# A list scheduler with new costs: a port lock, a delay between dependent operations, and query high parts on ScalarE

## The chip, the cores and the metric

The kernel runs on one core of one Trainium2 chip. The time is device microseconds of one execution. Five engines work beside each other, each through its own instructions in a fixed order: TensorE (PE, with its weight loads as PEld), VectorE (DVE), ScalarE (ACT), GpSimd (POOL) and SyncE (SP), which here mostly issues DMAs. An instruction whose operand is not ready holds up everything behind it on its engine. So the order that is written into the program decides who waits for whom.

## The reference, cut to what matters

```
scores = q @ k.T / 8 + bias            # 2 batches x 8 heads, 768 positions, head size 64
keep   = (key < n_global) or (0 <= query - key < n_local)
a      = exp(scores - max) / (sum + 1e-9)
x      = a @ v                          # 1536 tokens x 512
h      = relu(x @ w_in); x = (h * h) @ w_out           # 512 -> 2048 -> 512
xn     = x / sqrt(mean(x*x) + 1e-6) * rms_g
out    = (silu(xn @ w_gate) * (xn @ w_val)) @ w_out2   # 512 -> 1536 -> 512
```

## The kernel before, in words

Attention is cut into 16 slices: 4 chunks of 384 tokens times 4 pairs of heads. A slice has three tiles of 128 queries, 48 tiles in all. A tile runs through this chain: scores on PE (L931 in fp32 for the first eight slices, L939 from high and low parts for the last eight), bias and row minimum on DVE from PSUM (L949, with an accumulator read), exp with row sum on ACT (L953), sum plus 1e-9 on POOL (L957), reciprocal on DVE (L960), the scaling of one head on DVE and of the other on POOL (both L963), transposes on PE (L970), a copy to SBUF on ACT (L972), and the product with v on PE (L980). The result is split into a high part (ACT, L368) and a low part (DVE, L369).

For the last eight slices queries and keys, too, are split into high and low parts: `hi` writes high parts (L900, on the engine that QHI and KHI name), then DVE writes the low parts of the query (L888) and of the key (L891). Eight splits have two heads each, so there are 16 query high parts `qs` and 16 key high parts `kh`.

The weights are 68 blocks of 512 KB. Each comes by a DMA into `wraw`, and `expand` turns it into fp32 in `wbits`: one ACT instruction (L410) and four on DVE (L411, L413, L415, L418), each of which reads what the one before wrote. Then ACT writes the high part `M` (L368) and POOL or DVE the low part (L369). A matrix product is three PE instructions (L378 to L380: high by high, high by low, low by high). The first MLP follows each finished chunk (`first`: products, relu and square on ACT at L479 to L481, low part on DVE at L482), then the norm, then the gated MLP in Strassen-like products. Where PE would idle early on, short matmuls of ones fill the time (L1266).

The order is set by a planner, the class `Plan`. Every operation is recorded with its engine, a duration, the latency until another engine can use its result (`lat`), and what it reads and writes. `forward` is a list scheduler: it takes the ready operation with the earliest due time on the engine that is free first, and gives each a start. `solve` runs forward and backward several times and keeps the plan that ends first; `emit` then writes the instructions sorted by those starts. The durations are formulas (DVE, FAST, ACT, POOL1, POOL2). An operation with `port` set is one that uses the SBUF access shared by VectorE and GpSimd, and such operations were planned one after the other. POOL operations of the attention had `port=False`: the planner thought them free of it.

Of the kernel before, what the change touches and what calls it, by code (L numbers as in the profile page):

```python
# [16 lines left out]
ALU = mybir.AluOpType  # L17
# [35 lines left out]
AHEAD = (0, 0, 0, 3, 1, 1, 3, 3) + 8 * (1,)  # L53
QHI, KHI = "POOL", "POOL"
NSLACK = 0.5
# [18 lines left out]
class Plan:  # L74
# [33 lines left out]
    def solve(self):  # L108
        for o in reversed(self.ops):
            for q in o.succ:  # L110
                o.due = min(o.due, q.due - o.dur - (o.lat if q.eng != o.eng else 0.0))
        best = None
# [14 lines left out]
    def backward(self):  # L127
# [3 lines left out]
        for o in sorted(self.ops, key=lambda o: (-o.end, -o.n)):  # L131
            last = end
            for q in o.succ:
                last = min(last, q.late - (o.lat if q.eng != o.eng else 0.0))
            taken = busy.setdefault(o.eng, [])
            dur = o.end - o.start
            at = len(taken)
            for i, (a, b) in enumerate(taken):
                if b <= last - dur + 1.0e-9:
                    at = i  # L140
                    break
                last = min(last, a)
            taken.insert(at, (last - dur, last))
            o.late = last - dur
# [3 lines left out]
    def forward(self):  # L148
# [9 lines left out]
        while done < len(self.ops):  # L158
# [18 lines left out]
            else:  # L177
                o = heappop(ready[e])[2]
            if o.port:
                t = max(t, held)  # L180
# [19 lines left out]
            o.start = t  # L200
            o.end = t + o.dur + extra
            free[e] = o.end
            if o.port:
                held = o.end
            done += 1
            for q in o.succ:
                q.ready = max(q.ready, o.end + (o.lat if q.eng != e else 0.0))
                q.left -= 1
# [11 lines left out]

LAT = {"PE": 0.35, "DVE": 0.28, "ACT": 0.33, "POOL": 0.4, "SP": 2.6, "END": 0.0}
DVE = lambda n: 0.07 + n / 960
FAST = lambda n: 0.13 + n / 1920
ACT = lambda n: 0.07 + n / 1200
POOL1 = lambda n: 0.08 + n / 960
POOL2 = lambda n: 0.18 + n / 457
DMA = lambda kb: max(0.45, kb / 265.0)
# [34 lines left out]
class Mlp:  # L262
# [132 lines left out]
    def expand(self):  # L395
# [13 lines left out]
        bi = lambda: tl(bits).bitcast(I32)  # L409
        self.plan.add("ACT", ACT(512), lambda: nc.scalar.activation(tl(bits), f32(tl(raw)[:, :, 1]), AF.Abs), rr, rb)  # L410
        self.plan.add("DVE", FAST(512), lambda: v.tensor_scalar(  # L411
            out=tl(bits), in0=tl(bits), scalar1=LEAST, scalar2=MOST, op0=ALU.max, op1=ALU.min), rb, rb, port=True)
        self.plan.add("DVE", FAST(512), lambda: v.tensor_scalar(  # L413
            out=bi(), in0=bi(), scalar1=3, scalar2=0x3FFFFFF8, op0=ALU.logical_shift_left, op1=ALU.bitwise_and), rb, rb, port=True)
        self.plan.add("DVE", DVE(512) + 0.09, lambda: v.scalar_tensor_tensor(  # L415
            out=bi(), in0=tl(raw)[:, :, 0], scalar=29, in1=bi(), op0=ALU.logical_shift_right, op1=ALU.bitwise_or),
            rr + rb, rb, port=True)
        self.plan.add("DVE", DVE(512) + 0.09, lambda: v.scalar_tensor_tensor(  # L418
            out=bi(), in0=tl(raw)[:, :, 1], scalar=-(1 << 30), in1=bi(), op0=ALU.bitwise_and, op1=ALU.bitwise_or),
# [368 lines left out]
class Attention:  # L788
# [55 lines left out]
    def load(self, s):  # L844
# [18 lines left out]
        for j in range(2):  # L863
# [4 lines left out]
            if hp:  # L868
                self.op("POOL", 0.18 + CH / 985, lambda j=j, head=head: nc.gpsimd.tensor_scalar(
                    out=self.whole(s)[1][head, j], in0=self.whole(s)[1][head, j], scalar1=2.0 ** (2 * hp + j), scalar2=1.0,  # L870
                    op0=ALU.mult, op1=ALU.mult), [("qz", SLOTS[s])] + rq[j], rq[j], port=False)

    def split(self, s, kw):
# [9 lines left out]
        for j in range(2):  # L883
# [3 lines left out]
            self.hi(KHI, kw, lambda j=j: kh()[:, j, keys], lambda j=j: raw()[:, j, keys], 1.0, mine, [h] + whole)  # L887
            self.op("DVE", DVE(CH) + 0.09, lambda j=j, scale=scale: nc.vector.scalar_tensor_tensor(  # L888
                out=qs()[low, j], in0=raw()[low, j, KW:], scalar=scale, in1=f32(qs())[low, j],
# [5 lines left out]
    def hi(self, eng, n, out, src, scale, r, w):  # L895
# [3 lines left out]
        else:  # L899
            self.op(eng, 0.36 + n / 1830 if eng == "POOL" else FAST(n), lambda: self.mlp.eng(eng).tensor_scalar(  # L900
                out=out(), in0=src(), scalar1=scale, scalar2=1.0, op0=ALU.mult, op1=ALU.mult), r, w, port=eng == "DVE")

# [17 lines left out]
    def tile(self, n, due):  # L920
# [23 lines left out]
        for j in range(2):  # L944
# [398 lines left out]
```

## Time and profile before

| | us |
|---|---|
| median of 3 runs | 652.68 (652.17 to 653.1) |
| the profiled execution | 652.1 |
| its span, from the first instruction to the last | 650.2 |
| PE busy | 637.1 (98%) |
| DVE busy | 492.1 (76%) |
| ACT busy | 370.8 (57%) |
| POOL busy | 219.1 (34%) |

The 1.9 us between the span and the execution's time lie outside the program's instructions. The busy shares are averages over stages with different limits. A PE that is busy is not a PE at its peak, since the records of pipelined matmuls overlap. The rows that were read stage by stage stand further down.

### The profile page before, as it was taken

Reading aid. Unit: us, or ns where it says so; the run is one execution under the profiler, and the core shown is the slowest. Engines: PE = TensorE matmul, PEld = TensorE weight load, DVE = VectorE, ACT = ScalarE, POOL = GpSimd, SP = SyncE. Lnnn points to the kernel's source line nnn. Section 1 sums busy time; section 2 is a strip of 40 time slices with the busy share of each in tenths; the row PEclk is TensorE's granted clock in tenths of the full one; section 3 lists DMA queues with packets and bytes.
Section 4 is the critical chain, followed back from the end, with each engine's and each line's share of the span. In section 5 each row is a group of like instructions: output and inputs, shape, how many; then the busy total and the mean of one; then the engine's idle time right before and its main releaser. Section 6 shows DMA issues by size and latency. Waiting matters only on the chain.

```text
span 650.2 us, 10647 instructions
## 1 busy us (share of the span) xinstructions
PE 637.1 (98%) x3794; PEld 600.5 (92%) x3794; DVE 492.1 (76%) x1055; ACT 370.8 (57%) x834; POOL 219.1 (34%) x275
## 2 busy tenths in 40 slices
PE   8999999999999999999999999999999999999996
PEld 8788889899999999999999999999899999998995
DVE  6999998933888885237679998698878888887444
ACT  4779687766756564356656776654453443443310
POOL 5644666522332230024300212434454335351000
PEclk9999999999999999999999999999999999999998
DMA  8875676100333333002210110232121202310023
GB/s 228 234 234 152 195 180 168 49 25 7 125 123 104 99 118 109 0 1 76 87 34 1 33 33 1 66 105 89 38 94 66 98 32 77 119 65 1 2 85 115
DMA packets 20848, 56.38 MB, mean 87 GB/s; under 512 B 3248, under 2 KB 6064, under 8 KB 20784
## 3 DMA queue, kind: packets, MB, share of 16 engines
q1 hardware_dynamic: 19472, 53.82, 26.9%
q10 hardware_dynamic: 1312, 1.77, 0.8%
q8 instruction: 32, 0.52, 0.3%
q14 instruction: 32, 0.26, 0.1%
HBM read 52.43 MB, written 3.15 MB: 85 GB/s over the span
## 4 chain that ended last, share of the span: by engine, by line
PE 81%; DVE 12%; ACT 3%; DMA 2%; issue 1%; POOL 0%; SPq 0%; ACTq 0%; DVEq 0%; POOLq 0%
PE b L378 26%; PE b L379 26%; PE b L380 26%; DVE p L949 2%; DVE p L963 1%; PE tb L970 1%; PE av L980 1%; PE ps L939 1%; DVE kl L891 1%; DVE wbits L415 1%; DMA q<-in_kq_dram 1%; DVE wbits L418 1%; ACT p L953 1%; DVE wbits L413 1%; DMA k<-in_kq_dram 1%
## 5 line engine op out<-in xcount | busy, mean ns | idle before, releaser
L369 POOL TENSOR_TENSOR M<-wbits,M 128x512 fp32r<-128x512 f32 x60 | 82.0, 1372 | 226.5 <-ACT M L368 139.6
L378 PE MATMUL b<-xh,M 128*128 128x384 f32 x336 | 115.7, 344 | 0.5 <-DVE xl L369 0.5
L379 PE MATMUL b<-xl,M 128*128 128x384 f32 x336 | 112.8, 336 | 0.0
L380 PE MATMUL b<-xh,M 128*128 128x384 f32 x336 | 112.7, 335 | 0.0
L482 DVE TENSOR_TENSOR h<-ra,h 128x384 fp32r<-128x384 f32 x64 | 38.4, 604 | 44.7 <-ACT ra L481 44.5
L368 ACT CAST M<-wbits 128x512 fp32r<-128x512 f32 x68 | 41.8, 617 | 43.2 <-DVE wbits L418 29.9
L378 PEld LDWEIGHTS b<-xh,M 128*128 128x128 f32 x336 | 63.2, 188 | 2.7 <-DVE xl L369 0.8
L379 PEld LDWEIGHTS b<-xl,M 128*128 128x128 f32 x336 | 63.2, 188 | 1.9 <-DVE xl L369 0.3
L380 PEld LDWEIGHTS b<-xh,M 128*128 128x128 f32 x336 | 63.1, 188 | 0.2 <-DVE M L369 0.2
L378 PE MATMUL b<-h,M 128*128 128x384 f32 x176 | 61.0, 346 | 0.0
L665 DVE TENSOR_TENSOR y<-b,y 128x512 f32<-128x512 f32 (+1 forms) x61 | 41.2, 679 | 24.1 <-PE b L380 23.7
L379 PE MATMUL b<-h,M 128*128 128x384 f32 x176 | 59.1, 336 | 0.0
L380 PE MATMUL b<-h,M 128*128 128x384 f32 x176 | 59.0, 335 | 0.0
L380 PE MATMUL b<-M,h 128*128 128x512 f32 (+1 forms) x146 | 57.2, 392 | 0.0
L415 DVE SCALAR_TENSOR_TENSOR wbits<-wraw,wbits 128x512 int32<-128x512 int32 x68 | 56.1, 827 | 1.3
L379 PE MATMUL b<-M,h 128*128 128x512 f32 (+1 forms) x146 | 56.9, 390 | 0.0
L378 PE MATMUL b<-M,h 128*128 128x512 f32 (+1 forms) x146 | 56.8, 389 | 0.1
L953 ACT ACTIVATE p<-p,few 128x256 f32<-128x256 f32 (+1 forms) x96 | 46.4, 485 | 17.1 <-DVE few L949 13.9
L410 ACT ACTIVATE wbits<-wraw 128x512 f32<-128x512 f32 x68 | 45.1, 668 | 16.5 <-DMA wraw<-in_w_out_dram 8.5
L479 ACT ACTIVATE ra<-b 128x384 f32<-128x384 f32 x64 | 31.0, 486 | 39.6 <-PE b L380 39.4
L418 DVE SCALAR_TENSOR_TENSOR wbits<-wraw,wbits 128x512 int32<-128x512 int32 x68 | 50.3, 742 | 0.9
L411 DVE TENSOR_SCALAR wbits<-wbits 128x512 f32<-128x512 f32 x68 | 36.8, 541 | 9.7 <-ACT wbits L410 9.6
(137 smaller groups left out, 1616.5 us busy)
## 6 DMA issues: line engine op xcount, KB each, us to landing
wraw<-in_w_out_dram SPq DMA_DIRECT2D x28, 512.0 KB, 3.4
wraw<-in_w_in_dram SPq DMA_DIRECT2D x16, 512.0 KB, 3.5
wraw<-in_w_gate_dram SPq DMA_DIRECT2D x12, 512.0 KB, 3.3
wraw<-in_w_val_dram SPq DMA_DIRECT2D x12, 512.0 KB, 3.5
raw<-in_kq_dram SPq DMA_DIRECT2D x16, 240.0 KB, 4.8
raw<-in_kq_dram SPq DMA_DIRECT2D x16, 208.0 KB, 4.9
v<-in_vab_dram SPq DMA_DIRECT2D x8, 384.0 KB, 3.7
v<-in_vab_dram SPq DMA_DIRECT2D x8, 256.0 KB, 4.4
```

Of the source, the lines that this page charges most:

```text
L368: self.op("ACT", ACT(n), lambda: nc.scalar.copy(dst()[0], src()), rs, [(x, "hi") for x in ws])
L369: self.op(eng, t(n), lambda: e.tensor_tensor(out=dst()[1], in0=src(), in1=f32(dst()[0]), op=ALU.subtract), rs + [(x, "hi") for x in ws], [ ...
L378: nc.tensor.matmul(ps, lhsT=wh, rhs=ah, start=first, stop=False, skip_group_check=True)
L379: nc.tensor.matmul(ps, lhsT=wh, rhs=al, start=False, stop=False, skip_group_check=True)
L380: nc.tensor.matmul(ps, lhsT=wl, rhs=ah, start=False, stop=last, skip_group_check=True)
L410: self.plan.add("ACT", ACT(512), lambda: nc.scalar.activation(tl(bits), f32(tl(raw)[:, :, 1]), AF.Abs), rr, rb)
L411: self.plan.add("DVE", FAST(512), lambda: v.tensor_scalar(out=tl(bits), in0=tl(bits), scalar1=LEAST, scalar2=MOST, op0=ALU.max, op1=ALU.mi ...
L415: self.plan.add("DVE", DVE(512) + 0.09, lambda: v.scalar_tensor_tensor(out=bi(), in0=tl(raw)[:, :, 0], scalar=29, in1=bi(), op0=ALU.logica ...
L418: self.plan.add("DVE", DVE(512) + 0.09, lambda: v.scalar_tensor_tensor(out=bi(), in0=tl(raw)[:, :, 1], scalar=-(1 << 30), in1=bi(), op0=AL ...
L482: self.op("DVE", DVE(CH), lambda: nc.vector.tensor_tensor(out=get()[1], in0=t(), in1=f32(get()[0]), op=ALU.subtract), rt + hi, lo, port=True)
L665: self.op("DVE", DVE(a1 - a0), lambda o=o, ps=ps: nc.vector.tensor_tensor(out=o(), in0=ps(), in1=o(), op=ALU.add), [("b", bank)] + ro, ro)
L953: self.op("ACT", 0.29 + w / 1200, lambda j=j: nc.scalar.activation(tl(f"p{m}")[:, j, :w], tl(f"p{m}")[:, j, :w], AF.Exp, bias=tl("few")[:, ...
```

## The change

It has three parts. First, the planner's rules: a POOL operation with `port` now holds back or is held back through a lock that lies inside its own duration (it needs the lock `PRE` after its start and gives it back `POST` before its end), a dependent operation on the same engine is ready only `SAME` after the end of the one it reads (0.11 us on DVE, 0.12 on ACT, 0.08 on POOL, nothing on PE), and the POOL operations of the attention now have `port` set, all but L957. Second, new durations. Third, QHI names ACT: the 16 query high parts are written by an ACT instruction in place of a POOL one. What is computed stays the same. All lines from L226 on stand four lines lower in the changed kernel, so L963 is L967 there.

```
-QHI, KHI = "POOL", "POOL"
+QHI, KHI = "ACT", "POOL"
@@ solve, and backward in the same way
-                o.due = min(o.due, q.due - o.dur - (o.lat if q.eng != o.eng else 0.0))
+                o.due = min(o.due, q.due - o.dur - (o.lat if q.eng != o.eng else SAME[o.eng]))
@@ forward
-            if o.port:
+            lock = max(t + PRE, held) - t - PRE if o.port and e == "POOL" else 0.0
+            if o.port and e != "POOL":
                 t = max(t, held)
...
-            o.end = t + o.dur + extra
+            o.end = t + o.dur + extra + lock
             free[e] = o.end
             if o.port:
-                held = o.end
+                held = max(held, o.end - (POST if e == "POOL" else 0.0))
...
-                q.ready = max(q.ready, o.end + (o.lat if q.eng != e else 0.0))
+                q.ready = max(q.ready, o.end + (o.lat if q.eng != e else SAME[e]))
@@ durations
+SAME = {"PE": 0.0, "DVE": 0.11, "ACT": 0.12, "POOL": 0.08, "SP": 0.0, "END": 0.0}
+PRE, POST = 0.13, 0.12
-FAST = lambda n: 0.13 + n / 1920
+FAST = lambda n: 0.19 + n / 3600
-POOL2 = lambda n: 0.18 + n / 457
+POOL2 = lambda n: 0.14 + n / 461
+POOLS = lambda n: 0.25 + n / 1500
@@ hi (L900)
-            self.op(eng, 0.36 + n / 1830 if eng == "POOL" else FAST(n), lambda: self.mlp.eng(eng).tensor_scalar(
-                out=out(), in0=src(), scalar1=scale, scalar2=1.0, op0=ALU.mult, op1=ALU.mult), r, w, port=eng == "DVE")
+            self.op(eng, POOLS(n) if eng == "POOL" else FAST(n), lambda: self.mlp.eng(eng).tensor_scalar(
+                out=out(), in0=src(), scalar1=scale, scalar2=1.0, op0=ALU.mult, op1=ALU.mult), r, w, port=eng != "ACT")
@@ tile (L957, L960, L963)
-        self.op(EPS, 0.26, lambda: self.mlp.eng(EPS).tensor_scalar(
+        self.op(EPS, 0.19, lambda: self.mlp.eng(EPS).tensor_scalar(
...
-        self.op("DVE", 0.15, lambda: nc.vector.reciprocal(rs(), rs()), [("rs", m)], [("rs", m)])
+        self.op("DVE", 0.08, lambda: nc.vector.reciprocal(rs(), rs()), [("rs", m)], [("rs", m)])
...
-            self.op(e, 0.34 + w / 776 if e == "POOL" else FAST(w), lambda j=j, e=e: self.mlp.eng(e).tensor_scalar(
+            self.op(e, POOLS(w) if e == "POOL" else FAST(w), lambda j=j, e=e: self.mlp.eng(e).tensor_scalar(
...
-                op0=ALU.mult, op1=ALU.mult), [("rs", m), ("p", m, j)], [("p", m, j)], port=e != "POOL")
+                op0=ALU.mult, op1=ALU.mult), [("rs", m), ("p", m, j)], [("p", m, j)], port=True)
```

The new plan puts nearly everything in another order. Three places show how.

On VectorE, at the second weight block that is expanded, the kernel before has these rows. `p` are score tiles (a number for each of four buffers), `few` holds the row statistics, `wbits` and `wraw` the weight block, `M` its split form, and L949 with 128x1 is the accumulator read.

```order
L413 TENSOR_SCALAR wbits1_217<-wbits1_217 128x512
L960 RECIPROCAL few_157<-few_157 128x2
L949 ISA p2_181,few_157<-ps0_139,t00_148 128x128
L949 ISA few_157 128x1
L949 ISA p2_181,few_157<-ps0_139,t00_148 128x128
L949 ISA few_157 128x1
L963 TENSOR_SCALAR p0_156<-p0_156,few_157 128x256
L415 SCALAR_TENSOR_TENSOR wbits1_217<-wraw1_150,wbits1_217 128x512
L418 SCALAR_TENSOR_TENSOR wbits1_217<-wraw1_150,wbits1_217 128x512
L960 RECIPROCAL few_157<-few_157 128x2
L963 TENSOR_SCALAR p1_172<-p1_172,few_157 128x256
L369 TENSOR_TENSOR M0_260<-wbits0_154,M0_260 128x512
```

In the changed kernel the same part of VectorE's order, still with the first block, reads:

```order
L419 SCALAR_TENSOR_TENSOR wbits0_226<-wraw0_156,wbits0_226 128x512
L964 RECIPROCAL few_166<-few_166 128x2
L953 ISA p2_188,few_166<-ps0_141,t00_158 128x128
L953 ISA few_166 128x1
L967 TENSOR_SCALAR p0_165<-p0_165,few_166 128x256
L964 RECIPROCAL few_166<-few_166 128x2
L953 ISA p2_188,few_166<-ps0_141,t00_158 128x128
L953 ISA few_166 128x1
L967 TENSOR_SCALAR p1_176<-p1_176,few_166 128x256
L422 SCALAR_TENSOR_TENSOR wbits0_226<-wraw0_156,wbits0_226 128x512
```

Between a reciprocal and the scaling that reads it, and between two steps on one weight block, there now stands an operation on something else, often the bias operation that reads PSUM.

On ScalarE, in the first splits of the last eight slices (`qs` is a query high part, `raw` the loaded slice, `pt` the transposed tile, `y` the output of the first MLP, `xh` the high part of x), the kernel before has:

```order
L510 COPY y0_108<-b1_355 128x384
L972 COPY pt0_224<-tb_207 128x512
L510 COPY y0_108<-b2_415 128x384
L953 ACTIVATE p0_156,few_157<-p0_156,few_157 128x128 x2
L368 CAST xh2_498<-av_291 128x384
```

and the changed kernel:

```order
L514 COPY y0_109<-b1_424 128x384
L976 COPY pt0_224<-tb_214 128x512
L902 ACTIVATE qs0_798<-raw0_123 128x384
L514 COPY y0_109<-b2_487 128x384
L902 ACTIVATE qs1_857<-raw1_439 128x384
L414 ACTIVATE wbits0_226<-wraw1_221 128x512
L957 ACTIVATE p3_200,few_166<-p3_200,few_166 128x256 x2
L372 CAST xh2_477<-av_278 128x384
```

The query high parts stand ahead of exps, which come behind them in ScalarE's order.

On SyncE, at the start of the program (`k` and `q` are keys and queries of a slice, `raw0` at 64x384 queries of a later slice), the kernel before has:

```order
L861 DMA k0_81<-in_kq_dram 128x448
L407 DMA wraw0_93<-in_w_in_dram 128x1024
L866 DMA q1_86<-in_kq_dram 64x384 x2
L861 DMA k1_85<-in_kq_dram 128x448
L866 DMA raw0_104<-in_kq_dram 64x384
L407 DMA wraw1_150<-in_w_in_dram 128x1024
```

and the changed kernel:

```order
L865 DMA k0_81<-in_kq_dram 128x448
L865 DMA k1_85<-in_kq_dram 128x448
L870 DMA q1_86<-in_kq_dram 64x384 x2
L915 DMA v0_118<-in_vab_dram 128x128
L916 DMA v0_118<-in_vab_dram 128x512
L865 DMA k0_81<-in_kq_dram 128x448
L870 DMA raw0_123<-in_kq_dram 64x384 x2
L411 DMA wraw0_156<-in_w_in_dram 128x1024
```

Keys, queries and values of the first slices now go ahead of the first weight block, which was second in the queue and is eighth.

## Rows read from the trace of the kernel before

**Rows 1.** Busy time by stage: stretch, its length, then busy us (instructions) by engine.
```profile
core 0: us, PE busy (x) PEld busy (x) DVE busy (x) ACT busy (x) POOL busy (x), PEclk, DMA share, GB/s
0.00:10.00 10.00, 8.02 (x41) 7.67 (x42) 4.95 (x24) 3.04 (x7) 4.76 (x17) 1.00 0.74 194
10.00:50.00 40.00, 39.07 (x283) 33.14 (x282) 38.44 (x140) 31.97 (x100) 24.30 (x44) 1.00 0.84 241
50.00:90.00 40.00, 38.37 (x311) 34.50 (x310) 38.33 (x119) 31.91 (x94) 23.11 (x42) 1.00 0.62 176
90.00:130.00 40.00, 38.51 (x302) 34.82 (x301) 36.06 (x121) 31.74 (x95) 25.57 (x44) 1.00 0.44 119
130.00:150.00 20.00, 19.55 (x168) 17.79 (x166) 6.57 (x26) 12.34 (x35) 3.95 (x10) 1.00 0.07 21
150.00:370.00 220.00, 220.00 (x1263) 218.91 (x1264) 155.36 (x264) 132.07 (x259) 50.14 (x41) 1.00 0.21 68
370.00:400.00 30.00, 29.89 (x160) 27.18 (x159) 28.82 (x55) 23.68 (x45) 5.68 (x7) 1.00 0.06 19
400.00:650.20 250.20, 243.74 (x1279) 226.50 (x1278) 183.60 (x312) 104.08 (x206) 81.63 (x74) 0.99 0.20 68
```
**Rows 2.** Groups of PE instructions, 10 to 130 us: count, busy us, mean ns.
```profile
L1266 PE MATMUL b<-ones 128*128 128x128 f32 x40 | 5.8, 275 | 0.0
```
**Rows 3.** Timeline of VectorE, 16 to 21 us: start us, length us, instruction.
```profile
16.31 0.41 DVE L949 CUSTOM_DVE_ANT_0 p<-ps,rel 128x256 f32<-128x256 f32 x1
16.65 0.08 DVE L949 DVE_READ_ACCUMULATOR2_ANT few<- 128x1 f32 x1
...
17.00 0.42 DVE L411 TENSOR_SCALAR wbits<-wbits 128x512 f32<-128x512 f32 x1
17.45 0.62 DVE L413 TENSOR_SCALAR wbits<-wbits 128x512 int32<-128x512 int32 x1
...
20.19 0.16 DVE L960 RECIPROCAL few<-few 128x2 f32<-128x2 f32 x1
20.45 0.35 DVE L963 TENSOR_SCALAR p<-p,few 128x256 f32<-128x256 f32 x1
```
**Rows 4.** Groups of VectorE instructions, 0 to 150 us: count, busy us, mean ns.
```profile
L963 DVE TENSOR_SCALAR p<-p,few 128x256 f32<-128x256 f32 x40 | 15.9, 398 | 2.9
...
L888 DVE SCALAR_TENSOR_TENSOR qs<-raw,qs 64x384 fp32r<-64x384 f32 x16 | 9.6, 604 | 0.7 <-DVE p L963 0.3
...
L482 DVE TENSOR_TENSOR h<-ra,h 128x384 fp32r<-128x384 f32 x12 | 7.6, 630 | 1.8 <-ACT ra L481 1.8
...
L413 DVE TENSOR_SCALAR wbits<-wbits 128x512 int32<-128x512 int32 x11 | 6.1, 551 | 0.3
```
**Rows 5.** Single lines, 0 to 150 us: count, then ns min/median/max.
```profile
L963 DVE TENSOR_SCALAR p<-p,few x48: 270/353/801, 11.4 to 139.7; 128x256 f32<-128x256 f32 x40, 128x128 f32<-128x128 f32 x8
...
L888 DVE SCALAR_TENSOR_TENSOR qs<-raw,qs x16: 551/556/747, 59.4 to 124.7; 64x384 fp32r<-64x384 f32 x16
...
L482 DVE TENSOR_TENSOR h<-ra,h x12: 537/552/889, 52.7 to 132.5; 128x384 fp32r<-128x384 f32 x12
...
L369 DVE TENSOR_TENSOR xl<-av,xh x16: 530/550/557, 23.1 to 149.3; 128x384 fp32r<-128x384 f32 x16
...
L413 DVE TENSOR_SCALAR wbits<-wbits x11: 415/587/789, 12.3 to 82.7; 128x512 int32<-128x512 int32 x11
...
L949 DVE CUSTOM_DVE_ANT_0 p<-ps,rel x80: 402/417/426, 9.9 to 136.3; 128x256 f32<-128x256 f32 x80
...
L900 POOL TENSOR_SCALAR qs<-raw x16: 510/668/915, 54.8 to 123.1; 128x384 fp32r<-128x384 f32 x16
...
L957 POOL TENSOR_SCALAR few<-few x48: 191/242/763, 10.0 to 139.2; 128x2 f32<-128x2 f32 x48
...
L480 ACT ACTIVATE h<-ra x12: 513/526/544, 51.4 to 130.0; 128x384 fp32r<-128x384 f32 x12
```
**Rows 6.** Groups of GpSimd instructions, 0 to 150 us: count, busy us, mean ns.
```profile
L957 POOL TENSOR_SCALAR few<-few 128x2 f32<-128x2 f32 x48 | 15.6, 325 | 25.3 <-ACT p L953 23.1
...
L900 POOL TENSOR_SCALAR qs<-raw 128x384 fp32r<-128x384 f32 x16 | 10.8, 682 | 1.8 <-PE ps L931 0.9
```
**Rows 7.** Who waited for whom: us in total, times, longest us.
```profile
DVE few L960 <- POOL few L957: 2.3, 3, 1.6
...
ACT p L953 <- DVE few L949: 13.9, 18, 1.7
```
**Rows 8.** Timeline of SyncE at the start: issue us, length us, DMA.
```profile
1.19 0.42 SPq L407 DMA_DIRECT2D wraw<-in_w_in_dram  x1
...
2.90 0.59 SPq L861 DMA_DIRECT2D k<-in_kq_dram  x1
```
**Rows 9.** Timeline of VectorE: its first instruction on a weight block.
```profile
11.57 0.41 DVE L411 TENSOR_SCALAR wbits<-wbits 128x512 f32<-128x512 f32 x1
```

More of the change, by code (lines that the diff above doesn't have):

```diff
@@ L133, in backward @@
             for q in o.succ:
-                last = min(last, q.late - (o.lat if q.eng != o.eng else 0.0))
+                last = min(last, q.late - (o.lat if q.eng != o.eng else SAME[o.eng]))
             taken = busy.setdefault(o.eng, [])
@@ L409, in expand @@
         bi = lambda: tl(bits).bitcast(I32)
-        self.plan.add("ACT", ACT(512), lambda: nc.scalar.activation(tl(bits), f32(tl(raw)[:, :, 1]), AF.Abs), rr, rb)
+        self.plan.add("ACT", ACT(512) + 0.05, lambda: nc.scalar.activation(tl(bits), f32(tl(raw)[:, :, 1]), AF.Abs), rr, rb)
         self.plan.add("DVE", FAST(512), lambda: v.tensor_scalar(
@@ L414, in expand @@
             out=bi(), in0=bi(), scalar1=3, scalar2=0x3FFFFFF8, op0=ALU.logical_shift_left, op1=ALU.bitwise_and), rb, rb, port=True)
-        self.plan.add("DVE", DVE(512) + 0.09, lambda: v.scalar_tensor_tensor(
+        self.plan.add("DVE", DVE(512), lambda: v.scalar_tensor_tensor(
             out=bi(), in0=tl(raw)[:, :, 0], scalar=29, in1=bi(), op0=ALU.logical_shift_right, op1=ALU.bitwise_or),
             rr + rb, rb, port=True)
-        self.plan.add("DVE", DVE(512) + 0.09, lambda: v.scalar_tensor_tensor(
+        self.plan.add("DVE", DVE(512), lambda: v.scalar_tensor_tensor(
             out=bi(), in0=tl(raw)[:, :, 1], scalar=-(1 << 30), in1=bi(), op0=ALU.bitwise_and, op1=ALU.bitwise_or),
@@ L868, in load @@
             if hp:
-                self.op("POOL", 0.18 + CH / 985, lambda j=j, head=head: nc.gpsimd.tensor_scalar(
+                self.op("POOL", POOLS(CH), lambda j=j, head=head: nc.gpsimd.tensor_scalar(
                     out=self.whole(s)[1][head, j], in0=self.whole(s)[1][head, j], scalar1=2.0 ** (2 * hp + j), scalar2=1.0,
-                    op0=ALU.mult, op1=ALU.mult), [("qz", SLOTS[s])] + rq[j], rq[j], port=False)
+                    op0=ALU.mult, op1=ALU.mult), [("qz", SLOTS[s])] + rq[j], rq[j])
     def split(self, s, kw):
@@ L887, in split @@
             self.hi(KHI, kw, lambda j=j: kh()[:, j, keys], lambda j=j: raw()[:, j, keys], 1.0, mine, [h] + whole)
-            self.op("DVE", DVE(CH) + 0.09, lambda j=j, scale=scale: nc.vector.scalar_tensor_tensor(
+            self.op("DVE", DVE(CH) + 0.06, lambda j=j, scale=scale: nc.vector.scalar_tensor_tensor(
                 out=qs()[low, j], in0=raw()[low, j, KW:], scalar=scale, in1=f32(qs())[low, j],
```

## The prediction

> **What bounds the kernel now.** I read the busy time by stage first. From 150 to 370 us PE is busy for all of 220 us, and from 400 us on for 243.7 of 250.2 [rows 1]. In those stages hardly anything on another engine can shorten the run. PE has some room from 370 to 400 us, where the norm makes DVE the busiest but for PE (28.82 of 30). The stage that the change can reach is the attention. From 10 to 130 us DVE is busy 38.44 + 38.33 + 36.06 = 112.8 of 120 us, and ACT 95.6. PE shows 115.95, which hides that 40 of its instructions there are filler, 5.8 us [rows 1, 2]. So PE has 4.05 + 5.8 = 9.9 us in this stage that are not work. From 130 to 150 us it turns: DVE has 6.57 of 20 us and PE 19.55, so PE finishes the attention on its own pace. I conclude that DVE sets the pace for 120 us, that what is taken from it reaches the end only as far as PE can follow, and that PE can follow by at most 9.9 us plus what lies before 10 us.
>
> **What DVE loses its time to.** Two things, both without work in them. The first is back-to-back dependence. An independent successor starts before the end of the one before it: L949 at 16.31 ends at 16.72, and the next starts at 16.65, so -0.07 us. A dependent one starts after it: L411 ends at 17.42, L413 starts at 17.45, +0.03; the reciprocal ends at 20.35, the scaling that reads it starts at 20.45, +0.10 [rows 3]. One such pair costs 0.10 us in a weight block and 0.17 us at a reciprocal. The second is stretching beside GpSimd. The scaling on DVE takes 353 ns at the median and 801 at most, the shift L413 415 to 789, L482 537 to 889, L888 551 to 747, while L949, whose input is in PSUM, stays at 402 to 426 [rows 5]. With the means [rows 4] the four groups lose 40 x (398 - 353) + 11 x (551 - 415) + 12 x (630 - 537) + 16 x (604 - 551) ns = 1.8 + 1.5 + 1.1 + 0.8 = 5.2 us.
>
> **The change part by part.** *Order by dependence.* I counted pairs in the two orders, up to the last scaling: 35 reciprocals of the kernel before are followed at once by the scaling that reads them, 15 of the changed one; steps of one weight block stand next to each other 15 times before, 7 times after. That takes 20 x 0.17 + 8 x 0.10 = 4.2 us from DVE. Bounds: 0, if what now stands between waits for something itself, to 4.2. I take 4.2, since the nearest row, 16.65, shows no wait where L949 follows.
>
> *Query high parts on ScalarE.* 16 instructions leave GpSimd, 10.8 us with their stretching of 682 ns each on average [rows 6]. That is 15% of the 73.0 us that GpSimd is busy from 10 to 130 us [rows 1], so I take 15% of the 5.2 us of stretching, 0.8 us. ACT gets 16 instructions; its nearest row over 384 columns in SBUF is L480 at 526 ns [rows 5], so 8.4 us on 95.6 of 120, 87% busy after it. Exps and copies to SBUF are queued behind each of them, and an `h` high part or a transposed tile that comes late holds PE. Bounds: 0 to 8.4. Of ACT's waits the exps wait for DVE's L949 for 13.9 us [rows 7], so ACT mostly waits itself; I take a tenth, 0.8 us.
>
> *The lock in the plan.* The remaining 4.4 us of stretching go if GpSimd's operations fall beside DVE's PSUM operations. Nothing in a trace of before can say how well the executed times follow a plan; bounds are 4.4 gained and, should the new order collide more, 4.4 lost. I take half the gain, 2.2, as the plan of before had no lock for the attention's GpSimd operations at all, and they could hardly fall worse than by chance.
>
> *The shorter durations.* L957 is planned at 0.19 us (0.26 before) and still without the lock, but it takes 325 ns on average, 763 at most [rows 5, 6]. Behind it on GpSimd stand the scalings and key high parts; DVE's reciprocal waits for it and holds whatever follows in DVE's order. That wait was 2.3 us [rows 7]. Bounds of the added wait: 0, to 48 x (0.26 - 0.19) = 3.4 us; I take 1.2, about half of what is seen, since the plan of before was late there too.
>
> The Trainium skill, "SBUF — State Buffer", section "SBUF: two separate sides", calls the pair shared by VectorE and GpSimd an exclusive lock: who starts first has it for the whole instruction and the other fully blocks. By that rule L957 must take the lock like its neighbours, against this plan; the trace agrees (191 ns alone, 763 at most), and by the rule alone every L957 would be late by 325 - 190 ns, 6.5 us in 48, where my sum has 1.2.
>
> *SyncE at the start.* The first weight block goes from second in the queue (issued at 1.19 us) to eighth, and the second slice's keys from 2.90 us to the front [rows 8]. Before, DVE starts on a weight block at 11.57 us [rows 9]; now it must live on softmax work for longer. At most the 1.6 us that DVE is idle from 10 to 50 us are gained, and at most as many lost. I take 0; the cover is DVE's other 38.44 us.
>
> *The rest.* In 150 to 370 us PE is at 220 of 220; a new order there gives 0, and costs a stretched L482 (889 - 537 = 0.35 us) each time a low part of `h` is late. In the order in which the plan issues the work, such low parts stand one product ahead of their use 11 times in the second quarter of PE's products, where it was 4. With a few late that is up to 1 us; I take 0 and keep it for the range.
>
> **The sum.** DVE: 4.2 + 0.8 + 2.2 - 1.2 - 0.8 = 5.2 us. PE's 9.9 us can hold it, but PE's order is fixed too and the last 20 us are its own, so I let 85% through: 4.4 us. The profiled execution took 652.1 us, 0.6 under the median of before; 652.1 - 4.4 = 647.7 us.
>
> **The rivals.**
> A, *the runs do not follow the plan*: the stretching stays, apart from the part of the 16 moved instructions, and L957 comes late as above. For it: the durations of GpSimd scatter from 191 to 763 ns. Against it: every operation's start is bound to the same predecessors in plan and run. Then (4.2 + 0.8 - 1.2 - 0.8) x 0.85 = 2.6, and with the dependent pairs only half worth it 0.8: 651.3 to 649.5, say 650.4.
> B, *the shared access itself was the bound*: then taking 16 instructions of at least 510 ns from it [rows 5] gives 8.2 us whatever the order, within PE's 9.9: 643.9. For it: L413 at a median of 587 where 415 is possible. Against it: DVE's other rows are mostly at their minimum.
> The rule named above, one holder for a whole instruction, is what would bring this about.
> C, *slower: ScalarE becomes the bound*. 8.4 us come onto an engine with 24.4 free in 120 us, in bursts of two ahead of exps. It decides if ACT's free time lies in waits that remain, as the 13.9 us for L949 do: then 10.5 us are left, and bursts cannot use them. With all 8.4 on the path against 4.2 + 0.8 + 2.2 - 1.2 = 6.0 from DVE, and stalls of 1 us in the second quarter: +3.4, 655.5. Against it: DVE is ahead of ACT by 17 us of busy time today.
> D, *no change*: what DVE saves before 130 us PE spends after it, since its order puts first-MLP products between the last tiles: 652.1. For it: PE's 19.55 of 20 us there. Against it: the 9.9 us before.
>
> **How the numbers follow.** Chances: forecast 0.47 (its own range 645.5 to 650), A 0.17, B 0.12, C 0.12, D 0.12. This kernel's measurements can tell 0.2%, 1.3 us. Faster by more than that: the forecast, B and about two thirds of A, 0.70. Within it: D and part of A, 0.17. Slower: C and a little of D, 0.13. The range runs from a little under B, with the start's 1 us, 643.0, past D by 0.7 us, less than the 0.93 us between the three runs of before, 652.8.
>
> **What would show it.** Right: after the change the last low part of x (149.3 us now [rows 5]) comes some 4 us earlier, PE from there on is as before, DVE's L963 and L413 have means nearer 360 and 420 ns, and reciprocal and scaling have something between them. The L957 term is seen in what DVE's reciprocals wait for GpSimd, now 2.3 us. C would be seen in ACT over 95% busy from 60 to 120 us with DVE idle before L949 or the reciprocal. My sum is wrong if DVE gains and the attention's end does not move, or if PE is idle between 150 and 370 us.

## The result, and the profile after

The changed kernel takes 643.45 us (median of 4 executions, 642.54 to 643.89) against 652.57 (4, 652.17 to 653.1). The ratio is 0.9858, with a 95% interval of 0.9841 to 0.9875: 9.1 us less. The forecast of 647.7 us is 4.9 less, and the measured time lies below the forecast's own range (645.5 to 650), at the number of rival B (643.9). The profiled execution took 642.54 us with a span of 640.7.

Busy time by stage, kernel after; the columns are those of [rows 1], which is the same view of before.

```profile
0.00:10.00 10.00, 8.06 (x50) 7.88 (x51) 5.96 (x27) 3.39 (x10) 5.76 (x19) 1.00 0.76 199
10.00:50.00 40.00, 39.74 (x310) 35.13 (x309) 38.97 (x144) 35.95 (x109) 21.91 (x44) 1.00 0.84 253
50.00:90.00 40.00, 39.44 (x310) 36.00 (x310) 38.77 (x124) 35.61 (x105) 18.19 (x35) 1.00 0.64 182
90.00:130.00 40.00, 40.00 (x333) 37.73 (x330) 33.77 (x124) 35.07 (x107) 17.91 (x38) 1.00 0.40 111
130.00:150.00 20.00, 20.00 (x149) 18.84 (x148) 8.63 (x21) 13.28 (x31) 6.18 (x9) 1.00 0.07 22
150.00:370.00 220.00, 220.00 (x1267) 218.94 (x1266) 159.27 (x268) 129.59 (x254) 48.38 (x41) 1.00 0.21 68
```

PE is now busy for all of 90 to 150 us. From 150 to 370 us it was at 220 of 220 and still is, so nothing could be won there. ScalarE has 106.6 us in 10 to 130 us, where it had 95.6; GpSimd 58.0, where it had 73.0.

Single lines of the kernel after, 0 to 150 us (count, ns min/median/max, first and last start), beside [rows 5]. Lines from 226 on stand four further down than before: L949 is L953 now, L957 is L961, L963 is L967, L482 is L486, L413 is L417, L369 is L373, L888 is L892, and the query high parts are ScalarE's L902.

```profile
L373 DVE TENSOR_TENSOR xl<-av,xh x16: 530/550/559, 20.4 to 140.1; 128x384 fp32r<-128x384 f32 x16
...
L892 DVE SCALAR_TENSOR_TENSOR qs<-raw,qs x16: 551/555/636, 61.1 to 122.4; 64x384 fp32r<-64x384 f32 x16
...
L417 DVE TENSOR_SCALAR wbits<-wbits x13: 406/419/668, 15.0 to 149.2; 128x512 int32<-128x512 int32 x13
...
L967 DVE TENSOR_SCALAR p<-p,few x48: 272/354/595, 11.2 to 132.9; 128x256 f32<-128x256 f32 x40, 128x128 f32<-128x128 f32 x8
...
L902 ACT ACTIVATE qs<-raw x16: 506/527/566, 58.6 to 121.3; 128x384 fp32r<-128x384 f32 x16
...
L961 POOL TENSOR_SCALAR few<-few x48: 191/192/647, 9.5 to 131.9; 128x2 f32<-128x2 f32 x48
```

The last low part of x, the attention's end, starts at 140.1 us and not at 149.3: the whole gain, 9.2 us, lies before it. The weight blocks' shift (L417) is at 419 ns at the median, where it was 587 [rows 5].

Group means of VectorE in the same stretch, for [rows 4]:

```profile
L967 DVE TENSOR_SCALAR p<-p,few 128x256 f32<-128x256 f32 x40 | 16.7, 417 | 1.1
...
L486 DVE TENSOR_TENSOR h<-ra,h 128x384 fp32r<-128x384 f32 x16 | 9.0, 565 | 1.2 <-ACT ra L485 1.0
L892 DVE SCALAR_TENSOR_TENSOR qs<-raw,qs 64x384 fp32r<-64x384 f32 x16 | 8.9, 564 | 0.4
```

Two of them fell (630 to 565, 604 to 564), but the scaling rose, from 398 to 417 ns: the stretching did not simply go.

What PE's weight loads waited for, 10 to 130 us: us in total, times, longest. First before, then after.

```profile
PEld tb L970 <- ACT pt L972: 5.0, 9, 1.4
PEld ps L931 <- DVE few L949: 2.7, 8, 0.7
...
PEld ps L939 <- DVE few L949: 0.8, 2, 0.7
```

```profile
PEld tb L974 <- ACT pt L976: 0.9, 3, 0.4
PEld ps L935 <- DVE few L953: 0.7, 2, 0.4
```

The forecast did not use this view, and it shows where the 9 us were. All waits of weight loads listed in this stretch sum to 14.5 us before and 8.1 after; in 4.9 and 4.4 of these the profile shows nothing that was waited for ("issue"). The filler, which is no work either, falls from 5.8 us [rows 2] to 3.7:

```profile
L1270 PE MATMUL b<-ones 128*128 128x128 f32 x26 | 3.7, 275 | 0.0
```

With 1.1 us at the start (below) that is 6.4 + 2.1 + 1.1 = 9.6 us, near the 9.2 that the attention ends earlier. The largest part, 4.1 us, is transposes (`tb`) that waited for ScalarE's copy of a tile out of PSUM (`pt`). Here is the longest such wait of the kernel before (start us, length us; in brackets idle time before):

```profile
74.29 0.79 DVE L413 TENSOR_SCALAR wbits<-wbits 128x512 int32<-128x512 int32 x1
...
75.00 0.41 DVE L949 CUSTOM_DVE_ANT_0 p<-ps,rel 128x256 f32<-128x256 f32 x1
...
75.51 0.51 ACT L953 ACTIVATE p<-p,few 128x256 f32<-128x256 f32 x1 [1.92 <-POOL qs L900]
...
76.02 0.56 ACT L972 COPY pt<-tb 128x512 f32<-128x512 f32 x1
...
76.64 0.42 PEld L970 LDWEIGHTS tb<-ident,p 128*128 128x128 f32 x4 [1.40 <-ACT pt L972]
```

Read it from the end. PE waits 1.40 us for a copy. The copy stands on ScalarE behind an exp. ScalarE had been idle for 1.92 us before that exp. The profile names GpSimd's L900 as releaser, but the exp reads what VectorE's L949 wrote, which ended at 75.41. L949 was late behind a shift that took 0.79 us where 0.42 is possible. So a late VectorE instruction reaches PE by way of two queues. The stretched shift explains at most 0.37 of the 1.40 us; the rest it does not explain.

### The profile page after: what moved, and what is told of

The parts are those of the page before. It is cut to its first block, busy times and chain, and to the rows that moved or that the text cites. A ratio compares the mean times of both kernels' runs of the same rounds, so it can differ in the third digit from the quotient of the medians.

```text
span 640.7 us, 10669 instructions
## 1 busy us (share of the span) xinstructions
PE 631.4 (99%) x3790; PEld 599.2 (94%) x3790; DVE 490.5 (77%) x1055; ACT 371.3 (58%) x850; POOL 199.7 (31%) x259
## 4 chain that ended last, share of the span: by engine, by line
PE 81%; DVE 13%; DMA 2%; issue 1%; ACT 1%; POOL 0%; SPq 0%; ACTq 0%; DVEq 0%; POOLq 0%
PE b L383 25%; PE b L382 25%; PE b L384 25%; DVE p L953 2%; PE av L984 2%; PE tb L974 2%; PE ps L943 1%; DVE p L967 1%; DVE xl L373 1%; DVE wbits L419 1%; DMA raw<-in_kq_dram 1%; DVE wbits L422 1%; DVE wbits L417 1%; DVE wbits L415 1%; DMA q<-in_kq_dram 1%
## 5 line engine op out<-in xcount | busy, mean ns | idle before, releaser
L373 POOL TENSOR_TENSOR M<-wbits,M 128x512 fp32r<-128x512 f32 x60 | 81.4, 1362 | 256.3 <-ACT M L372 217.9
L486 DVE TENSOR_TENSOR h<-ra,h 128x384 fp32r<-128x384 f32 x64 | 36.9, 578 | 28.9 <-ACT ra L485 28.4
L419 DVE SCALAR_TENSOR_TENSOR wbits<-wraw,wbits 128x512 int32<-128x512 int32 x68 | 58.0, 853 | 1.2
L415 DVE TENSOR_SCALAR wbits<-wbits 128x512 f32<-128x512 f32 x68 | 37.9, 558 | 20.6 <-ACT wbits L414 19.8
L957 ACT ACTIVATE p<-p,few 128x256 f32<-128x256 f32 (+1 forms) x96 | 46.7, 490 | 11.4 <-DVE few L953 9.3
L422 DVE SCALAR_TENSOR_TENSOR wbits<-wraw,wbits 128x512 int32<-128x512 int32 x68 | 50.8, 746 | 0.8
```

Source lines behind the costliest of these rows:

```text
L373: self.op(eng, t(n), lambda: e.tensor_tensor(out=dst()[1], in0=src(), in1=f32(dst()[0]), op=ALU.subtract), rs + [(x, "hi") for x in ws], [ ...
L415: self.plan.add("DVE", FAST(512), lambda: v.tensor_scalar(out=tl(bits), in0=tl(bits), scalar1=LEAST, scalar2=MOST, op0=ALU.max, op1=ALU.mi ...
L419: self.plan.add("DVE", DVE(512), lambda: v.scalar_tensor_tensor(out=bi(), in0=tl(raw)[:, :, 0], scalar=29, in1=bi(), op0=ALU.logical_shift ...
L422: self.plan.add("DVE", DVE(512), lambda: v.scalar_tensor_tensor(out=bi(), in0=tl(raw)[:, :, 1], scalar=-(1 << 30), in1=bi(), op0=ALU.bitwi ...
L486: self.op("DVE", DVE(CH), lambda: nc.vector.tensor_tensor(out=get()[1], in0=t(), in1=f32(get()[0]), op=ALU.subtract), rt + hi, lo, port=True)
L957: self.op("ACT", 0.29 + w / 1200, lambda j=j: nc.scalar.activation(tl(f"p{m}")[:, j, :w], tl(f"p{m}")[:, j, :w], AF.Exp, bias=tl("few")[:, ...
```

## The experiments

The plan fixes each engine's order, so I could keep an order and change one thing in it, or change one rule and plan again. Theory 1, that of the forecast: order by dependence, the lock in the plan and the changed start together make VectorE faster. Theory 2: the access shared by VectorE and GpSimd was the bound, and 16 instructions leaving it are the gain (rival B; its 643.9 us is the time that was measured). Theory 3: any new plan differs by chance. From the second group on also theory 4, the lock is the largest part, and theory 5, delay and lock help only together.

All ratios are against runs of the kernel before (652.3 to 652.6 us at the median). "Lost on PE" is filler plus all waits of weight loads from 10 to 130 us.

| kernel | us | ratio, 95% interval | last low part starts | lost on PE |
|---|---|---|---|---|
| before | 652.57 | | 149.3 | 5.8 + 14.5 = 20.3 |
| after | 643.45 | 0.9858 [0.9841, 0.9875] | 140.1 | 3.7 + 8.1 = 11.8 |
| x1, order of before, query parts on ScalarE | 652.34 | 0.9999 [0.999, 1.0009] | 149.6 | 5.8 + 14.8 = 20.6 |
| x2, order of after, query parts on GpSimd | 646.55 | 0.9914 [0.9897, 0.993] | 144.0 | 3.7 + 11.4 = 15.1 |
| x3, new rules, query parts on GpSimd | 645.94 | 0.9901 [0.9885, 0.9918] | 143.6 | 4.3 + 11.2 = 15.5 |
| x4, old rules, query parts on ScalarE | 652.15 | 0.9995 [0.9986, 1.0005] | 149.5 | 6.2 + 14.0 = 20.2 |
| x5, after without the delay | 654.17 | 1.0024 [1.0014, 1.0033] | 147.1 | 3.7 + 17.1 = 20.8 |
| x6, after with the old lock | 649.89 | 0.9969 [0.9958, 0.9981] | 147.8 | 5.0 + 14.1 = 19.1 |
| x7, after with the old durations | 642.29 | 0.9843 [0.9826, 0.9859] | 139.1 | 5.3 + 5.7 = 11.0 |
| x8, after, first weight block early | 644.69 | 0.9885 [0.9869, 0.9902] | 141.9 | 4.8 + 8.6 = 13.4 |
| x9, after, lock on L961 too | 644.76 | 0.9882 [0.9865, 0.9898] | 143.3 | 5.5 + 9.3 = 14.8 |
| x10, before with the delay alone | 648.39 | 0.9938 [0.9922, 0.9955] | 144.4 | 5.6 + 12.9 = 18.5 |
| n1, before, one planned duration 1 ns longer | 650.93 | 0.9976 [0.9967, 0.9986] | 147.8 | 5.0 + 13.4 = 18.4 |
| n2, after, the same 1 ns | 643.07 | 0.986 [0.9843, 0.9876] | 140.3 | 4.0 + 7.3 = 11.3 |

**Order or engine: x1, x2.** Each keeps one kernel's order, places and waits and moves only the 16 query high parts to the other engine.

x1, on the kernel before:

```diff
-            self.hi(QHI, CH, lambda j=j: qs()[:, j], ...
+            self.hi("POOL/ACT", CH, lambda j=j: qs()[:, j], ...
+        if eng == "POOL/ACT":
+            self.op("POOL", 0.36 + n / 1830, lambda: nc.scalar.activation(out(), src(), AF.Copy, scale=scale), r, w, port=False)
```

> Kernel before, its plan and every order kept, only the 16 query high parts are issued on ScalarE at the places that they had on GpSimd. Theory 1 (the order by dependence, the start and the plan make the gain, the engine of the high parts little): 650.5 to 653.5 us, as ScalarE's new instructions stand where nobody planned them. Theory 2 (the access shared by VectorE and GpSimd was the bound, and 16 instructions of 0.51 us taken from it are the gain): 644 to 646 us, whatever the order. Theory 3 (any new plan scatters by several us, and this one was lucky): says nothing here, since the plan is the same.

652.34: no gain in time. VectorE is relieved all the same. Group means of x1, 0 to 150 us:

```profile
L965 DVE TENSOR_SCALAR p<-p,few 128x256 f32<-128x256 f32 x40 | 15.6, 389 | 2.7
...
L888 DVE SCALAR_TENSOR_TENSOR qs<-raw,qs 64x384 fp32r<-64x384 f32 x16 | 9.6, 604 | 0.8 <-DVE p L965 0.3
...
L482 DVE TENSOR_TENSOR h<-ra,h 128x384 fp32r<-128x384 f32 x12 | 6.9, 572 | 4.1 <-ACT ra L481 4.1
```

L888 keeps the 604 ns of [rows 4], but L482 falls from 630 to 572 and the scaling from 398 to 389. All of VectorE's instructions up to the attention's end take 2.1 us less together, nearly what they lose in the kernel after (2.3). The time comes back as waiting: L482 waits 4.1 us for ScalarE, where it waited 1.8. Theory 2, a gain whatever the order, falls, although its number was the one that matched. x1 alone does not show what the relief would be worth without ScalarE's new work at unplanned places; x4, where that work is planned, gains nothing either.

x2, on the kernel after:

```diff
-            self.hi(QHI, CH, lambda j=j: qs()[:, j], ...
+            self.hi("ACT/POOL", CH, lambda j=j: qs()[:, j], ...
+        if eng == "ACT/POOL":
+            self.op("ACT", ACT(n), lambda: nc.gpsimd.tensor_scalar(
+                out=out(), in0=src(), scalar1=scale, scalar2=1.0, op0=ALU.mult, op1=ALU.mult), r, w)
```

> Changed kernel, its plan and every order kept, only the 16 query high parts are issued on GpSimd again, at the places that they have on ScalarE. Theory 1: 644 to 646.5 us, most of the gain stays. Theory 2: 650 to 652.5 us, the 8.2 us are gone again. Theory 3: as theory 1.

646.55, just over theory 1's range: the new order keeps 5.9 of its 9 us even with the work on the old engine. The engine is worth 3.1 us in this order and nothing in the old one. Part of the 3.1 may be that GpSimd here has work at places that were planned for ScalarE.

**Rules or engine, planned anew: x3, x4.** The same split, but with a plan made for it. x3 is the kernel after, x4 the kernel before:

```diff
-QHI, KHI = "ACT", "POOL"
+QHI, KHI = "POOL", "POOL"
```

> Changed kernel with the query high parts on GpSimd and planned there: the new rules and durations alone. Theory 1: 643.5 to 646.5 us; reciprocals followed at once by their scaling are 12 in its order (15 in the changed kernel, 35 before). Theory 2: 650 to 652.5 us. Theory 3: anywhere from 643 to 652.

```diff
-QHI, KHI = "POOL", "POOL"
+QHI, KHI = "ACT", "POOL"
```

> Kernel before with the query high parts planned on ScalarE by the old rules and durations: the third part alone. Theory 1: 649.5 to 653 us; its order has 39 reciprocals followed at once by their scaling. Theory 2: 644 to 646 us. Theory 3: anywhere from 643 to 655.

x3 gains 6.5 us, x4 nothing (its interval holds 1). The rules and durations carry the change; the engine adds 2.5 us, and only with them.

**Which rule: x5, x6, x7, x10.** The first three each take one part out of the kernel after; x10 puts the delay alone into the kernel before.

x5:

```diff
-SAME = {"PE": 0.0, "DVE": 0.11, "ACT": 0.12, "POOL": 0.08, "SP": 0.0, "END": 0.0}
+SAME = {"PE": 0.0, "DVE": 0.0, "ACT": 0.0, "POOL": 0.0, "SP": 0.0, "END": 0.0}
```

> Changed kernel planned without the delay between dependent operations of one engine (SAME all zero), lock and durations as changed. Its order has 37 reciprocals followed at once by their scaling, 17 pairs of steps of one weight block (15 and 7 in the changed kernel). Theory 1 (the delay in the plan is the largest single part): 646.5 to 648.5 us, 3 to 5 us lost, with the small gaps on VectorE back to about 5 us. Theory 4 (the lock in the plan is the largest part): 643 to 645 us.

654.17, worse than before, 10.7 us worse than after and outside both ranges. Two stages of x5:

```profile
10.00:50.00 40.00, 36.50 (x282) 30.77 (x280) 35.43 (x134) 32.03 (x102) 22.14 (x44) 1.00 0.91 230
...
150.00:370.00 220.00, 218.69 (x1252) 216.59 (x1251) 152.91 (x260) 128.03 (x252) 45.76 (x38) 1.00 0.20 67
```

From 10 to 50 us PE is busy 3.2 us less (36.50 against 39.74), and x5 loses time behind the attention too: 505.7 us from the end of the last low part of x to the last instruction, where after has 500.1, before 500.4, and no other kernel over 502.8. There PE waits for low parts of `h`, 2.5 of these 5.6 us. Waits of x5, 150 to 372 us:

```profile
PEld b L383 <- DVE h L486: 2.5, 4, 1.5
```

That is the stall which the forecast kept for the second quarter; in the kernel after no such wait stands there.

The 10.7 us are no clean price of the delay. The changed kernel plans some instructions shorter than before (the reciprocal at 0.08 us in place of 0.15, the last two steps on a weight block by 0.09 us each), so x5 has neither the delay nor the longer durations, and its order has slightly more close pairs than that of before (37 and 17, where the forecast counted 35 and 15). The kernel after with old durations and no delay was not run.

x6:

```diff
-            lock = max(t + PRE, held) - t - PRE if o.port and e == "POOL" else 0.0
-            if o.port and e != "POOL":
+            lock = 0.0
+            if o.port:
...
-                held = max(held, o.end - (POST if e == "POOL" else 0.0))
+                held = o.end
...
-                op0=ALU.mult, op1=ALU.mult), [("rs", m), ("p", m, j)], [("p", m, j)], port=True)
+                op0=ALU.mult, op1=ALU.mult), [("rs", m), ("p", m, j)], [("p", m, j)], port=e != "POOL")
```

Two more GpSimd operations of the attention, among them the key high parts, lose their `port` in the same way.

> Changed kernel planned with the lock of the kernel before (GpSimd's operations of the attention free of it), delay and durations as changed. Theory 1: 644 to 646 us; the stretching of VectorE up to the attention's end goes from 9.6 us to about 11.3. Theory 4: 647 us or more, with stretching well over 12 us.

649.89, within theory 4's time and not theory 1's, so the lock in the plan is worth 6.4 us here. But not as less stretching: over all of VectorE's records up to the attention's end, the time above the undisturbed length (for each group of lines the 5th percentile in before) is 10.7 us in x6 and 9.6 in after. Theory 4's stretching of well over 12 us did not come either. VectorE's idle time in gaps longer than 0.13 us is 22.2 against 16.0. PE's waits sum to nearly those of before. Waits of x6, 10 to 130 us:

```profile
ACT p L957 <- DVE few L953: 11.9, 14, 2.3
PEld tb L974 <- ACT pt L976: 5.3, 8, 1.0
```

In the kernel after, over the same stretch, the exps wait for VectorE for 5.2 us and not 11.9:

```profile
ACT p L957 <- DVE few L953: 5.2, 11, 1.0
```

These waits go with the time here, but neither is its measure: in x3 the exps wait 13.5 us over this stretch, in x4 the transposes wait only 1.8 us for copies, and the times are 645.94 and 652.15. Only the sum in the table's last column goes with the time.

x7 takes before's planned durations, such as

```diff
-FAST = lambda n: 0.19 + n / 3600
+FAST = lambda n: 0.13 + n / 1920
...
-        self.op(EPS, 0.19, lambda: self.mlp.eng(EPS).tensor_scalar(
+        self.op(EPS, 0.26, lambda: self.mlp.eng(EPS).tensor_scalar(
```

> Changed kernel planned with the durations of the kernel before, delay and lock as changed. Its order has 6 reciprocals followed at once by their scaling and no pair of steps of one weight block. Theory 1: 643 to 646 us, the durations matter little. Theory 4: the same; a theory that the durations made the gain: 649 us or more.

642.29, the lowest time of all and just under theory 1's range; its interval overlaps that of after, so the two are not told apart. Against before it is faster by 1.6% (1.4 to 1.7). Nothing shows that the new durations gave anything.

x10, on the kernel before:

```diff
-                q.ready = max(q.ready, o.end + (o.lat if q.eng != e else 0.0))
+                q.ready = max(q.ready, o.end + (o.lat if q.eng != e else SAME[e]))
...
+SAME = {"PE": 0.0, "DVE": 0.11, "ACT": 0.12, "POOL": 0.08, "SP": 0.0, "END": 0.0}
```

> Kernel before with the delay between dependent operations alone put into its planner; lock, durations and query high parts as before. Its order has 9 reciprocals followed at once by their scaling and 1 pair of steps of one weight block. Theory 1 (the delay is the largest single part): 646.5 to 649 us. Theory 5 (delay and lock help only together): 650 us or more.

648.39: the delay alone gives 4.0 us. Without the delay the other parts give nothing (x5); without the lock 2.4 us (x6); with both 9.1. The parts do not add, as the 10.7 and 6.4 us of taking each out show. Theory 5 falls for the delay, which helps alone. The lock was never run alone, since x5 has the shorter durations beside it, so for the lock theory 5 stays open. Theory 4 missed x5 by 9 us and falls as it was put. Which of the two is larger is not settled: up to the attention's end x5 loses 7.0 us against after and x6 7.7 (last low part at 147.1 and 147.8, after 140.1).

**The start: x8.** Order and plan of after; only the first weight block's DMA goes second on SyncE again.

```diff
-        todo = [(o.start, 1, o.n, o.emit) for o in self.ops]
+        todo = [(0.01 if o is self.early else o.start, 1, o.n, o.emit) for o in self.ops]
...
-        self.plan.add("SP", DMA(512), lambda: nc.sync.dma_start(
+        load = self.plan.add("SP", DMA(512), lambda: nc.sync.dma_start(
...
+        if n == 0:
+            self.plan.early = load
```

> Changed kernel, its plan and every order kept, except that the DMA of the first weight block is issued second on SyncE, as in the kernel before. Theory 1 (the start gives 1.1 us, as the queries and the counts land sooner without the 512 KB ahead of them): 644 to 645 us, first bias operation at about 8.6 us in place of 7.6. If the start is hidden: 643.4 us as the changed kernel.

644.69: 1.2 us slower, and none of its executions is as fast as the slowest of after (644.19 against 643.89). VectorE's conversion of the counts and its first bias, in before, after and x8:

```profile
5.38 0.17 DVE L1077 CAST nf<-nw 128x4 f32<-128x4 int32 x1 [2.52 <-DMA nw<-in_counts_dram]
...
8.65 0.29 DVE L949 CUSTOM_DVE_ANT_0 p<-ps,t 128x128 f32<-128x128 f32 x1 [0.98 <-PE ps L931]
```

```profile
4.56 0.30 DVE L1081 CAST nf<-nw 128x4 f32<-128x4 int32 x1 [1.70 <-DMA nw<-in_counts_dram]
...
7.58 0.28 DVE L953 CUSTOM_DVE_ANT_0 p<-ps,t 128x128 f32<-128x128 f32 x1
```

```profile
4.76 0.17 DVE L1083 CAST nf<-nw 128x4 f32<-128x4 int32 x1 [1.90 <-DMA nw<-in_counts_dram]
...
8.90 0.29 DVE L955 CUSTOM_DVE_ANT_0 p<-ps,t 128x128 f32<-128x128 f32 x1 [1.76 <-PE ps L937]
```

The first bias starts at 8.90 us instead of 7.58, because the first scores wait for queries. DMAs of queries issued in the first 9 us (count, size, median us from issue to landing), in after and x8:

```profile
q<-in_kq_dram ACTq DMA_DIRECT2D x2, 96.0 KB, 4.7
q<-in_kq_dram SPq DMA_DIRECT2D x2, 96.0 KB, 4.6
```

```profile
q<-in_kq_dram ACTq DMA_DIRECT2D x2, 96.0 KB, 6.3
q<-in_kq_dram SPq DMA_DIRECT2D x2, 96.0 KB, 6.4
```

With the 512 KB under way the queries take 1.6 to 1.8 us longer to land, also those that ScalarE's queue issues and that do not stand behind the block. Of the 1.3 us at the first bias, 1.2 are seen at the end.

**L961 under the lock: x9.**

```diff
-            [("sm", m, 0), ("sm", m, 1)], [("rs", m)], port=False)
+            [("sm", m, 0), ("sm", m, 1)], [("rs", m)], port=True)
```

> Changed kernel with the lock given to L957 (now L961), too, the one GpSimd operation of the attention that was planned free of it. If its late ends cost what the prediction charged for them, 642 to 643 us; if nothing waited for them, 643 to 645 us, as the changed kernel within what another plan makes.

644.76: no gain. But this rule did not take away the wait that I had charged. VectorE's reciprocals waiting for L961, 0 to 150 us, in after, x9 and x7:

```profile
DVE few L964 <- POOL few L961: 2.1, 4, 1.1
```

```profile
DVE few L964 <- POOL few L961: 4.4, 7, 1.1
```

```profile
DVE few L964 <- POOL few L961: 1.0, 3, 0.6
```

In x9 the wait is longer than in after, so x9 says only that planning these instructions under the lock did not help. What the wait costs stays open.

**Chance: n1, n2.** In the kernel before (n1) and after (n2):

```diff
-DVE = lambda n: 0.07 + n / 960
+DVE = lambda n: 0.071 + n / 960
```

> Kernel before with one constant of its planner moved by 1 ns (VectorE's 0.07 us to 0.071): a new plan with no new knowledge in it. Theory 1 (the rules make the difference): 650.5 to 654 us. Theory 3 (any new plan scatters by several us): outside that, as far as 645 or 658.

> Changed kernel with the same constant moved by 1 ns. Theory 1: 642 to 645.5 us. Theory 3: outside that.

Both came within theory 1's range. A new plan by chance alone moved the time by 1.4 us on the old rules and by 0.4 on the new. Delay, lock and rules are well above that. The 1.3 us of x9 and the 1.2 of x7 are not, so no more is read from them than that nothing was gained or lost for certain. x8 kept the plan and needs no such allowance. One perturbation of each kernel is a small sample, and theory 3 is refuted only as an explanation of the whole.

## Why the prediction was right about the direction and half right about the size

*The stage.* Right. All of the gain lies before the attention's end, PE is unchanged from 150 to 370 us, and no stall by low parts of `h` came.

*The terms on VectorE.* Every kernel here runs the same 426 VectorE instructions up to the end of the last low part of x. The time to that end is made of their lengths, the gaps of up to 0.13 us between them less their overlaps, and the longer idle times. Against the kernel before, in us:

| kernel | lengths | gaps less overlaps | longer idle | attention's end |
|---|---|---|---|---|
| after | -2.3 | -3.6 | -3.3 | -9.2 |
| x1, query parts moved, old order | -2.1 | -0.6 | +3.0 | +0.3 |
| x2, query parts back, new order | 0.0 | -3.8 | -1.6 | -5.3 |
| x5, no delay | -1.8 | +1.2 | -1.5 | -2.1 |
| x6, old lock | -1.1 | -3.2 | +2.8 | -1.5 |
| x10, delay alone | +0.4 | -6.2 | +0.8 | -4.9 |

The forecast had 4.2 for the gaps, 3.0 for the lengths (0.8 and 2.2) and 2.0 of added waiting (1.2 and 0.8). The first two are near what came. The waiting has the wrong sign: it fell by 3.3 us, about 1.1 of it at the start, where the first bias comes earlier. A 1 ns change moved each column by 1.5 to 1.6 us in the old plan (n1), so smaller differences between two plans are not read.

*Order by dependence, 4.2 us.* Right. Gaps of up to 0.13 us on VectorE fall from 93 to 65, by as many as the 28 pairs counted. They and the overlap of neighbours give 1.7 + 1.9 = 3.6 us, and the delay alone moves the same column by 6.2 (x10). The forecast's example of an overlap (16.65 in [rows 3]) was no independent pair, since that row is L949's read of its own accumulator; the rows here are such pairs. After, an independent operation stands between reciprocal and scaling (timeline of VectorE):

```profile
26.36 0.15 DVE L964 RECIPROCAL few<-few 128x2 f32<-128x2 f32 x1
26.43 0.53 DVE L373 TENSOR_TENSOR xl<-av,xh 128x384 fp32r<-128x384 f32 x1
26.89 0.27 DVE L967 TENSOR_SCALAR p<-p,few 128x128 f32<-128x128 f32 x1
27.08 0.42 DVE L417 TENSOR_SCALAR wbits<-wbits 128x512 int32<-128x512 int32 x1
```

The reciprocal is overlapped by 0.08 us, where before the scaling started 0.10 behind it [rows 3], and shift and scaling both run at their undisturbed length.

*The lock in the plan, 2.2 us: the step that failed.* I took it for a matter of stretching, of which 4.4 us were left, and took half. The lengths fell by 2.3 us with both causes together, and the scaling's mean, which I expected near 360 ns, rose to 417; only the shift's came near its 420, from 551 to 438. But taking the lock out costs 6.4 us (x6), and of the 7.7 us at the attention's end 6.1 are longer idle time on VectorE, 1.2 are lengths. So the term was in the wrong place: less in how long an operation takes than in when its result is there for the next engine. How the lock in the plan brings this about was not tested. In my reading [rows 7] the exps' 13.9 us of waiting for L949 stood only as a sign that ScalarE had room; from 0 to 141 us it is 9.3 in the kernel after. Followed one queue further, as in the wait at 76.64 us, it can lead to the copies and to the 5.0 us for which transposes waited.

*Query high parts on ScalarE, 0.8 gained and 0.8 lost.* Right in sum for the old order, where x1 and x4 measure nothing; too little for the new, where they are worth 2.5 to 3.1 us (x2, x3). ScalarE took 16 instructions of 527 ns, and its exps wait less, so the cost that I charged did not come. The swap shortens VectorE's instructions by 2.1 us in the old order (x1) and by 2.3 in the new (x2 against after), so VectorE is relieved in both. In the old order longer idle time takes it back, as the table shows. That another place was late first there is my reading and was not tested.

*The shorter durations, 1.2 us lost.* Open. VectorE's reciprocals wait 2.1 us for L961 (2.3 before), whose mean is 259 ns (325 before), so nothing was added against before. But with the old durations (x7) the wait is 1.0 and the run 1.2 us shorter, the size that I charged, and within what another plan makes. The Trainium skill, "SBUF — State Buffer", section "SBUF: two separate sides", would have L961 take the pair's lock like its neighbours. The trace agrees that it can be held up (191 to 647 ns), but planning it under the lock gave nothing (x9).

*SyncE at the start, 0.* Too low by 1.2 us (x8). I looked for the cost of a later weight block and not for the loads that its transfer held up.

*The 85% and PE's 9.9 us.* Wrong on both sides. All 9.2 us at the attention's end reached the end of the run, and PE's room was larger than I read. PE's busy share showed 4.05 us idle in 10 to 130 us; the weight loads waited for 14.5 there. The profile models the ends of matmuls, so a PE shown as busy could still be held up, and filler plus weight-load waits (20.3 us) was the better figure. Over the fourteen kernels it goes roughly with the time; x5, with its loss behind the attention, is the exception.

*The rivals.* B met the number by chance and is refuted by x1: it would have needed the gain in any order. A missed the time (649.5 to 651.3), and x6 shows that the run answers to the plan, with 6.4 us; but its premise, that the stretching stays, came true in the main: 9.6 us of it are left, by the measure used for x6. C fell with ScalarE, busy for 51.60 of the 60 us from 60 to 120 us (86%, where C would need 95%), and its exps wait less for VectorE than before. D fell with the attention's end.

What stays open: how x2's and x3's extra waits split between GpSimd's load and the order, what the lock gives alone, what the shorter durations cost, and how wide the scatter of plans is beyond one sample each.

## What to carry to other kernels

A planner's cost model paid where it told of waits that the runs show (a dependent successor, a lock); that corrected durations paid was not seen. The lock's gain appeared more as less waiting than as shorter operations. So follow the late result through the engines to the one that sets the end, and read that engine's room from the sum of its waits, not from its busy share and not from one wait. Instructions can get shorter and the run not: in x1 the saving came back as idle time. A rival whose number matches may still be wrong: keep the order and move the one thing, and learn from a 1 ns change how far plans scatter before a part is believed.

## What the runs showed of the hardware that I had not expected

GpSimd's relief reached VectorE and not the end: with 16 instructions fewer beside it in the same order (x1), VectorE's 426 instructions took 2.1 us less together, though one group, L888, kept its mean of 604 ns, and the run took as long as before. And one weight block of 512 KB among the first loads made the queries land 1.6 to 1.8 us later, also those issued on another engine's queue. It delayed the first bias by 1.3 us, of which 1.2 were still there at the end of a run of 643 us (x8).
